# Grouped-query attention over a cached sequence on one core: the output in two PSUM banks, two copies and one store of whole rows

## The chip, the cores and the metric

The kernel runs on one NeuronCore of a Trainium2 chip. The metric is the device time of one execution in microseconds (us). Besides that time there is a profile of one execution, taken by the hardware profiler; its span runs from the first to the last instruction and is a little shorter than the time of the same execution.

The core has these engines: TensorE (PE, with its weight loads as PEld), VectorE (DVE), ScalarE (ACT), GpSimd (POOL) and SyncE (SP), which here only issues transfers. SBUF is the memory of 128 partitions that all engines read; PSUM, in eight banks per partition, receives what TensorE computes.

## The reference

```python
B, Sq, D = 8, 4, 512
Hq, Hkv, Sk, Dh = 32, 8, 2048, 128
rep = Hq // Hkv                                    # 4 query heads share a head of K and V
q = (x @ wq).reshape(B, Sq, Hq, Dh).transpose(0, 2, 1, 3)
k = jnp.repeat(k_cache, rep, axis=1)
v = jnp.repeat(v_cache, rep, axis=1)
scores = jnp.einsum("bhqd,bhkd->bhqk", q, k) * (Dh ** -0.5)
p = softmax(scores, axis=-1)
o = jnp.einsum("bhqk,bhkd->bhqd", p, v)
return o.transpose(0, 2, 1, 3).reshape(B, Sq, Hq * Dh) @ wo
```

Everything is bf16. The caches are 33.6 MB each, wq and wo 4.2 MB each; x and the output are 32 rows (8 sequences of 4 tokens) of 512 columns, 32 KB.

## The kernel before

The work is cut into 8 units: two groups of four K/V heads, times four pairs of sequences. For each unit the kernel loads 4 MB of K and 4 MB of V into one of four slots of a ring in SBUF (`load_kv`), turns K with VectorE's transposes (`turn`), computes the scores into a tile `s_ps` of four PSUM banks (`scores`), takes the maximum (`top`) and the exponentials (`exps`), turns the weights (`weights`) and multiplies them by V (`values`). The results of a unit are scaled, joined and sorted by tokens (`scaled`, `joined`, `by_tokens`). When a group of heads is complete, `to_rows` copies it out of two PSUM tiles, the first half with ScalarE, the second with VectorE, into one SBUF tile, and turns it into `oP[gg]`, in which each of 16 steps r holds 128 rows of the last product's inner dimension by 32 tokens.

The last product is `project`: for each step r and each half of the 512 output columns it multiplies `oP[gg][:, r, :]` (128 x 32) by 256 columns of wo. The first half goes to partitions 0 to 31 and the second to partitions 32 to 63 of `out_ps`, which is a view of bank 0 of `s_ps`, 256 columns wide; each half is a sum over 32 matmuls. wo is the last load, in seven pieces that get smaller towards the end (`load_wo`, L113), so that the last matmuls wait for a piece of 128 KB. Then one ScalarE copy (L409) brings the 64 x 256 sums as bf16 into `out_sb`, and SP issues one transfer (L411) that writes them. Since the halves of a row lie on different partitions, this transfer names the output as 2 x 32 rows of 256 columns, 512 bytes each.

Instructions are issued in the order of the program on each engine's own queue; an engine waits on semaphores that a planner derives from the tiles that instructions read and write. SP's queue holds all but two of the loads, and the store behind them. The waits in that queue (for a slot of the ring to come free) set when loads start. Nothing comes behind the store but the end of the program (L437 in the profile).

Of the kernel before, what the change touches and what calls it, by code (L numbers as in the profile page):

```python
# [8 lines left out]
BF16 = mybir.dt.bfloat16  # L9
# [8 lines left out]
def kernel(  # L18
# [9 lines left out]
    nc = tc.nc  # L28

    B, Sq, D = x.shape  # L30
# [4 lines left out]
    T = B * Sq  # L35
# [14 lines left out]
    DH = D // 2  # L50
# [6 lines left out]
    const = ctx.enter_context(tc.tile_pool(name="const", bufs=1))  # L57
# [19 lines left out]
    q_bd = [const.tile([128, NB, J * 2, G, NB, Q], BF16, name=f"q_bd{i}") for i in range(2)]  # L77
    p_bd = [const.tile([128, CH // 2, G, 32, 2], BF16, name=f"p_bd{i}") for i in range(4)]
    oP = [const.tile([128, RW, T], BF16, name=f"oP{i}") for i in range(NG)]
    out_sb = const.tile([2 * T, DH], BF16, name="out_sb")  # L80

    units = [(gg, bp) for gg in range(NG) for bp in range(NP)]
    slot_of = {}
# [67 lines left out]
    for r, b in ((r, b) for r in range(rep) for b in range(NB)):  # L151
        nc.gpsimd.tensor_copy(
            out=perm[:, r, 32 - NB * Sq :]
            .rearrange("k (g x) -> k g x", g=G)[:, :, : NB * Sq]
            .rearrange("k g (b s) -> k b g s", b=NB)[:, b],
            in_=by_row[:, r, b],
        )
    for b in range(NB):
        nc.vector.tensor_reduce(
            out=of_b[:, b : b + 1],  # L160
            in_=ident[:, :].rearrange("k (g b q) -> k b g q", g=G, b=NB)[:, b],
# [27 lines left out]
    s_ps = psum_s.tile([128, NT, 512], FP32, name="s_ps")  # L189
# [138 lines left out]
    def project(gg, r0, r1):  # L328
        w = ring[:, slot_of["wo"], gg, :].rearrange("p (r j) -> p r j", r=RW)
        for r in range(r0, r1):  # L330
            for half in range(2):
                nc.tensor.matmul(
                    out_ps[half * T : (half + 1) * T, :],
                    lhsT=oP[gg][:, r, :],
                    rhs=w[:, r, half * DH : (half + 1) * DH],
                    start=(gg == 0 and r == 0),
                    stop=(gg == NG - 1 and r == RW - 1),
                )
# [9 lines left out]
    for gg in range(NG):  # L348
        psq = psum_o.tile([128, rep * Dh], FP32, tag="o", name="psq")
        for r in range(R):  # L350
# [10 lines left out]
            out=q_sb[:, gg, :, :, :, :].rearrange("t r j w e -> t (r j w e)"), in_=psq[:, :]  # L361
        )
        for i in range(rep):
            nc.vector.transpose(  # L364
                out=qT[:, gg, :, :, i, :, :].rearrange("w j b s e -> w j b (s e)").bitcast(FP32),
                in_=q_sb[:, gg, i, :, :, :].rearrange("t j w e -> t (j w e)").bitcast(FP32),
            )
    queries(0)

    out_ps = s_ps[: 2 * T, 0, :DH]  # L370
    for u in range(NU + 1):
        if u < NU:
            for t in range(NT):
# [19 lines left out]
        if u >= 1:  # L393
# [5 lines left out]
            if u == NU:  # L399
                joined(u - 1)  # L400
                by_tokens(u - 2)
        issue(2 + 2 * u)
    project(0, 0, 4)
    by_tokens(NU - 1)
    to_rows(NG - 1, RW // 4)
    project(0, 4, RW)
    project(1, 0, RW)
    assert not loads
    nc.scalar.copy(out=out_sb[:, :], in_=out_ps)  # L409
    rows = out.flatten_outer_dims().rearrange("t (h n) -> h t n", h=2)  # L410
    nc.sync.dma_start(out=rows, in_=out_sb[:, :])  # L411


# [28 lines left out]
```

## Time and profile before

| | us |
|---|---|
| three runs | 185.8, 191.71, 191.63 (median 191.63) |
| profiled execution, its own time | 185.8 |
| span of the profiled execution | 183.9 |
| PE busy | 133.3 (72% of the span) |
| DVE busy | 127.3 (69%) |
| ACT busy | 74.1 (40%) |
| POOL busy | 37.7 (20%) |
| HBM read | 75.53 MB, 411 GB/s over the span |
| ScalarE's copy of the output, L409 | 0.366 |
| SP's issue of the store, L411 | 0.675 |

The mean granted TensorE clock of the profiled execution is 0.976. The times of the engines add up instructions that run beside each other; what sets the end is read from the chain of waits, which follows the last instruction back to what released it, and from the transfers.

These are the rows of the projection, by line: durations in ns (smallest, median, largest), first and last start in us, operand shapes.

```profile
L332 PEld LDWEIGHTS <-oP x64: 92/97/97, 175.3 to 179.9; 128*32 128x32 bf16 x64
L332 PE MATMUL s_ps<-ring,oP x64: 269/273/283, 175.3 to 179.9; 128*32 128x256 bf16 x64
```

The 64 matmuls of both groups stand between 175.3 and 179.9 us; the spacing of their starts is much closer than the duration of one, since they are pipelined.

### The profile page before, as it was taken

The page shows a single profiled execution, that of the slowest core. Times are in us where ns is not written, and L with a number is a line of the kernel's source. Part 1 is how long each engine was busy: PE and PEld are TensorE (multiplying, and loading weights), DVE is VectorE, ACT ScalarE, POOL GpSimd, SP SyncE. Part 2 cuts the span into 40 slices and gives each one's busy share as a digit, 9 for nine tenths or more (in the row PEclk, how much of TensorE's full clock was granted, in tenths as well). Part 3 has the DMA queues.
Part 4 walks back from the last instruction along what each step waited for, and adds up shares of the span by engine and source line. Part 5 has one row for each costly group of instructions (what it writes and reads, how often), then busy time and mean ns, then how long its engine had stood idle before and what let it go on. Part 6 is the DMA issues. An engine that isn't in the chain of part 4 may idle for free.

```text
span 183.9 us, 2334 instructions
## 1 busy us (share of the span) xinstructions
PE 133.3 (72%) x900; PEld 81.4 (44%) x900; DVE 127.3 (69%) x160; ACT 74.1 (40%) x91; POOL 37.7 (20%) x98
## 2 busy tenths in 40 slices
PE   0000079901999699978996898789788968899991
PEld 0000023300358335833782377238633853398870
DVE  6527029068975997499749965997898579769140
ACT  2000020049506940793099009902980297037010
POOL 8700033008001700260034004300520040005000
PEclk9999999995699999999999999999999999999997
DMA  6999999999999999999999999999999999999980
GB/s 271 410 435 420 435 421 438 424 438 438 424 435 421 435 424 440 417 440 435 424 431 420 442 424 433 442 413 438 420 442 428 431 435 420 421 426 424 428 316 8
DMA packets 6109, 75.71 MB, mean 412 GB/s; under 512 B 498, under 2 KB 850, under 8 KB 1106
## 3 DMA queue, kind: packets, MB, share of 16 engines
q1 hardware_dynamic: 5810, 71.37, 91.1%
q10 hardware_dynamic: 288, 4.19, 5.4%
q8 instruction: 7, 0.11, 0.2%
q14 instruction: 4, 0.03, 0.0%
HBM read 75.53 MB, written 0.03 MB: 411 GB/s over the span
## 4 chain that ended last, share of the span: by engine, by line
DVE 37%; DMA 25%; PE 19%; ACT 9%; issue 3%; SPq 2%; POOL 2%; DVEq 0%; ACTq 0%; POOLq 0%
DVE kt L172 23%; DMA ring<-in_wo_dram 14%; PE s_ps L195 13%; DMA ring<-in_wq_dram 11%; ACT p_sb L229 8%; DVE stat L208 8%; PE o_ps L269 4%; DVE pt L243 2%; DVE stat L260 2%; PE psq L353 2%; SPq L113 2%; POOL p_bd L253 1%; DVE stat L216 1%; DVE o_sb L287 1%; POOL q_bd L184 1%
## 5 line engine op out<-in xcount | busy, mean ns | idle before, releaser
L195 PE MATMUL s_ps<-kt,q_bd 128*128 128x512 bf16 x256 | 67.4, 395 | 24.3 <-POOL q_bd L184 16.3
L172 DVE STREAM_TRANSPOSE kt<-ring 128x1024 f32<-128x1024 f32 x64 | 73.8, 1207 | 5.5 <-DMA ring<-in_k_cache_dram 5.2
L269 PE MATMUL o_ps<-ring,p_bd 128*128 128x256 bf16 x512 | 57.0, 273 | 0.0
L195 PEld LDWEIGHTS <-q_bd 128*128 128x128 bf16 x256 | 24.7, 99 | 66.1 <-issue 23.6
L269 PEld LDWEIGHTS <-p_bd 128*128 128x128 bf16 x512 | 49.8, 98 | 5.9
L229 ACT ACTIVATE p_sb<-s_ps,stat 128x1024 bf16<-128x1024 f32 x16 | 22.0, 1399 | 65.3 <-DVE stat L216 65.3
L253 ACT COPY p_bd<-pt 32x1024 bf16<-32x1024 bf16 x44 | 45.8, 1041 | 1.3 <-DVE pt L243 0.8
L253 POOL COPY p_bd<-pt 32x1024 bf16<-32x1024 bf16 x16 | 17.0, 1063 | 112.0 <-DVE pt L243 109.5
L208 DVE TENSOR_REDUCE stat<-s_ps 128x1 f32<-128x1024 f32 x16 | 18.8, 1219 | 12.2 <-PE s_ps L195 12.2
L243 DVE STREAM_TRANSPOSE pt<-p_sb 128x512 f32<-128x512 f32 x16 | 11.4, 711 | 16.1 <-ACT p_sb L229 16.0
L184 POOL COPY q_bd<-qT 32x64 bf16<-32x64 bf16 x64 | 13.1, 230 | 19.4 <-DVE qT L364 17.6
L344 PE MATMUL xtp<-ident,x_sb 32*128 32x32 bf16 x4 | 0.3, 194 | 14.1 <-DMA x_sb<-in_x_dram 14.1
L353 PE MATMUL psq<-ring,xT_sb 128*32 128x512 bf16 x32 | 3.6, 629 | 8.2 <-DMA ring<-in_wq_dram 8.2
L364 DVE STREAM_TRANSPOSE qT<-q_sb 128x64 f32<-128x64 f32 x8 | 1.2, 213 | 8.9 <-ACT q_sb L360 8.9
L146 DVE MEMSET p_bd<- 128x2048 uint32 x3 | 5.3, 1765 | 2.0 <-PEq L426 1.2
L344 PEld LDWEIGHTS <-x_sb 32*128 32x128 bf16 x4 | 0.2, 117 | 14.1 <-DMA x_sb<-in_x_dram 14.1
L260 DVE TENSOR_SCALAR stat<-of_b,stat 128x2 f32<-128x2 f32 x8 | 5.9, 733 | 0.3
L287 DVE SCALAR_TENSOR_TENSOR o_sb<-o_ps,stat,o_sb 128x128 bf16<-128x128 f32 x8 | 2.5, 316 | 4.8 <-ACT o_sb L281 4.8
L353 PEld LDWEIGHTS <-xT_sb 128*32 128x32 bf16 x32 | 1.3, 139 | 9.7 <-issue 9.2
L360 ACT CAST q_sb<-psq 128x512 bf16<-128x512 f32 x2 | 1.2, 586 | 10.9 <-PE psq L353 10.9
L281 ACT ACTIVATE o_sb<-o_ps,stat 128x128 bf16<-128x128 f32 x8 | 2.9, 368 | 5.6 <-PE o_ps L269 5.4
L347 ACT COPY xT_sb<-xtp 128x128 bf16<-128x128 bf16 x1 | 0.3, 266 | 11.5 <-PE xtp L344 11.5
(26 smaller groups left out, 38.4 us busy)
## 6 DMA issues: line engine op xcount, KB each, us to landing
ring<-in_k_cache_dram SPq DMA_DIRECT2D x6, 4096.0 KB, 22.0
ring<-in_v_cache_dram SPq DMA_DIRECT2D x5, 4096.0 KB, 25.3
ring<-in_v_cache_dram SPq DMA_DIRECT2D x6, 2048.0 KB, 27.1
ring<-in_k_cache_dram SPq DMA_DIRECT2D x3, 2048.0 KB, 25.4
ring<-in_wo_dram SPq DMA_DIRECT2D x3, 1024.0 KB, 25.6
ring<-in_k_cache_dram ACTq DMA_DIRECT2D x1, 2048.0 KB, 12.1
ring<-in_wq_dram ACTq DMA_DIRECT2D x1, 2048.0 KB, 20.2
ring<-in_wq_dram SPq DMA_DIRECT2D x1, 2048.0 KB, 20.9
```

Source lines behind the costliest of these rows:

```text
L146: nc.vector.memset(t[:, :, :, :, :], 0.0)
L172: nc.vector.transpose(out=kt[:, :, :, :, :].rearrange("w c j s e -> w (c j s e)").bitcast(FP32), in_=ring[:, slot_of["k", u], b, t * n : ( ...
L184: nc.gpsimd.tensor_copy(out=qb[rows, b, :, g, b, :].rearrange("w (j e) q -> w j e q", e=2), in_=qT[rows, gg, :, NB * bp + b, :, :, :].rear ...
L195: nc.tensor.matmul(s_ps[:, t, :], lhsT=q_bd[u % 2][:, b, 2 * j + e, :, :, :].rearrange("w g b q -> w (g b q)"), rhs=kts[u, b, t][:, :, j, ...
L208: nc.vector.tensor_reduce(out=stats[u][0][:, h : h + 1], in_=s_ps[:, 2 * h : 2 * h + 2, :].rearrange("q t n -> q (t n)"), axis=AX, op=ALU.max,
L229: nc.scalar.activation(out=p_sb[:, :, :, :].rearrange("q c s e -> q c e s"), in_=s_ps[:, 2 * h : 2 * h + 2, :].rearrange("q t (c e s) -> q ...
L243: nc.vector.transpose(out=pt[:, :, :, :].rearrange("s c q e -> s (c q e)").bitcast(FP32), in_=ps[u, h][:, :, :, :].rearrange("q c s e -> q ...
L253: copy(out=pb[rows, :, g, :, :], in_=pt[rows, :, :, :])
L260: nc.vector.tensor_scalar_mul(stats[u][3][:, :], of_b[:, :], stats[u][4][:, :])
L269: nc.tensor.matmul(o_pss[u][:, :, :], lhsT=pbs[u, h][:, i // 2, :, :, i % 2].rearrange("s g q -> s (g q)"), rhs=v[:, :, h * CH + i, :], st ...
L287: nc.vector.scalar_tensor_tensor(out=o_sb[:, 1, :], in0=o_pss[u][:, 1, :], scalar=stats[u][3][:, 1:2], in1=o_sb[:, 0, :], op0=ALU.mult, op ...
L353: nc.tensor.matmul(psq[g * T : (g + 1) * T, :], lhsT=xT_sb[:, r, :], rhs=w[:, (gg * G + g) * rep * Dh : (gg * G + g + 1) * rep * Dh], star ...
```

## The change

`out_ps` becomes a list of two views: the first half stays on partitions 0 to 31 of bank 0 of `s_ps`, the second goes to partitions 32 to 63 of bank 1. `out_sb` becomes 32 rows of 512 columns. ScalarE copies the first half into its left columns, VectorE the second half (from partitions 32 to 63 to partitions 0 to 31) into its right columns, and one transfer writes 32 rows of 1024 bytes.

```diff
-    out_sb = const.tile([2 * T, DH], BF16, name="out_sb")
+    out_sb = const.tile([T, D], BF16, name="out_sb")
...
                 nc.tensor.matmul(
-                    out_ps[half * T : (half + 1) * T, :],
+                    out_ps[half],
                     lhsT=oP[gg][:, r, :],
...
-    out_ps = s_ps[: 2 * T, 0, :DH]
+
+    out_ps = [s_ps[h * T : (h + 1) * T, h, :DH] for h in range(2)]
...
-    nc.scalar.copy(out=out_sb[:, :], in_=out_ps)
-    rows = out.flatten_outer_dims().rearrange("t (h n) -> h t n", h=2)
-    nc.sync.dma_start(out=rows, in_=out_sb[:, :])
+    nc.scalar.copy(out=out_sb[:, :DH], in_=out_ps[0])
+    nc.vector.tensor_copy(out=out_sb[:, DH:], in_=out_ps[1])
+    nc.sync.dma_start(out=out.flatten_outer_dims(), in_=out_sb[:, :])
```

In the changed kernel the three last statements are lines L410, L411 and L412.

## The prediction

> **What bounds the kernel now.** I read the page first (span, busy tenths, transfer rate), then the end of the chain of waits, then the timeline, the queue's waits and the transfers of the last microseconds, because the change touches only what stands behind the last matmuls.
>
> The page:
>
> ```profile
> span 183.9 us, 2334 instructions
> ...
> DMA  6999999999999999999999999999999999999980
> GB/s 271 410 435 420 435 421 438 424 438 438 424 435 421 435 424 440 417 440 435 424 431 420 442 424 433 442 413 438 420 442 428 431 435 420 421 426 424 428 316 8
> DMA packets 6109, 75.71 MB, mean 412 GB/s; under 512 B 498, under 2 KB 850, under 8 KB 1106
> ```
>
> From the second slice to the third from the end the transfer engines are busy at 410 to 442 GB/s: the kernel is bound by reading its 75.5 MB, and nothing in the change reads a byte more or less. Only the last slice moves almost nothing (8 GB/s). The chain of waits from 179 us on:
>
> ```profile
> 153.61 25.58 DMA ring<-in_wo_dram
> 179.19 0.04 issue
> 179.23 0.62 PE s_ps L332 x6
> 179.85 0.01 issue
> 179.86 0.30 PE s_ps L332 x2
> 180.16 0.02 issue
> 180.19 0.37 ACT out_sb L409
> ```
>
> The last piece of wo lands, eight matmuls of 256 columns finish the output, ScalarE copies it. Then the timeline (start, duration), SP's own waits, and the transfers of the window 181 to 183.9 us (40 slices of 0.0725 us):
>
> ```profile
> 180.58 0.68 SPq L411 DMA_DIRECT2D out_dram<-out_sb  x1
> ```
>
> ```profile
> SPq L437 <- DMA out_dram<-out_sb: 1.5, 1, 1.5
> ```
>
> ```profile
> DMA  0000000000001101111111110000000000000000
> GB/s 0 0 0 0 0 0 0 0 0 0 0 7 28 14 14 42 42 49 42 42 42 42 42 42 0 0 0 0 0 0 0 0 0 0 0 0 0 0 0 0
> DMA packets 66, 0.03 MB, mean 11 GB/s; under 512 B 2, under 2 KB 66, under 8 KB 66
> ```
>
> So the tail behind the last matmul is 180.16 to 183.91, 3.75 us: hand-over and copy 0.42, issue 0.68, 0.54 until the first packet (slice 11, 181.80), packets until slice 23 ends (182.74, so 0.94), and 1.17 for the last hand-over and the barriers that close the program. The store runs on few transfer engines: the busy share is one tenth of 16, at 42 GB/s. The two packets under 512 B say how few. The program has 31 loads, and the page counts 498 such short packets: 31 x 16 + 2. I read them as one completion write for each transfer engine that takes part, 16 for every load, also for x (32 rows of 1024 bytes), and 2 for this store of 2 x 32 rows of 512 bytes. So 64 packets go through two engines, 32 in a row each, at 0.94 / 32 = 29 ns.
>
> **The change, part by part.** All against the profiled execution, whose own time is 185.8 us: span 183.9 and 1.9 around it. The median of the three runs shown is 191.63; two of them lie within 0.1 of it, 5.9 us above the profiled one, and no trace shows where. The change's difference is worked out in the profiled one and carried over to both.
>
> *Two banks.* The second half's matmuls go to the next bank, on the same 32 partitions as before. Number, shapes and order of PE's instructions stay, and so do their waits. The two halves already lie on different partitions, and in the stretch of 41 such matmuls at 176.73 they come every 2.46 / 41 = 60 ns, under the 97 ns of a weight load: two streams overlap now. Only the last pair is in the open; it could gain at most one such step (0.06) or lose a whole matmul if pairs stopped overlapping (0.27). I take 0, since pace and operands are the same. Both banks were last read for these columns by L229 of the last unit, from 163.74 to 165.14, ten microseconds before the first write at 175.34.
>
> *Copies.* ScalarE's copy keeps 256 columns; with 128 partitions (L321) it takes 0.372, with 64 (L409) 0.366, so with 32 it stays at 0.37. VectorE gets a copy of 256 columns from PSUM, whose nearest row is:
>
> ```profile
> L321 DVE CAST q_sb<-o_pm_e x2: 416/420/425, 127.7 to 176.5; 128x256 bf16<-128x256 f32 x2
> ```
>
> 0.42 us. It reads partitions 32 to 63 and writes 0 to 31, which no row does; L321's 0.42 is the nearest, and the 0.35 of the 128-column L287 bounds it below. Do the copies run side by side? In the order of the changed kernel's instructions, VectorE's copy (now L411) waits for ScalarE's counter alone, at 74, the value that the copy of L410 sets; and the store waits for VectorE's. So they run one after the other. Behind VectorE's wait stands only the end of the program (its last transposes ended at 178.4); SP, with the store, waits for it. Hand-over from ScalarE to VectorE: 0.03 (L281 ends at 175.64, L287 starts at 175.67). Added to the path: 0.03 + 0.42 = 0.45. If they overlapped, VectorE alone would end at 180.61 instead of 180.56: 0.05.
>
> The Trainium skill, page "PSUM — Partial Sum Buffer", section "Specifications (TRN2)", says that ScalarE and VectorE can read PSUM in parallel at full rate as long as their banks differ; by that alone the added term would be 0.05, not 0.45. Nothing in the trace before has two such copies on one output, and the listed wait decides for me.
>
> *Issue.* SP's issue of the old store took 0.675. The nearest row for the new one is the load of x, of the very same 32 rows of 1024 bytes on both sides: 0.406 (all loads of the ring that waited for nothing: 0.33 to 0.61). I take 0.41: a gain of 0.27, bounds 0 and 0.34.
>
> *Transfer.* 32 packets of 1024 bytes on 16 engines, as for x: two each. The step of 29 ns for 512 bytes gives 58 for 1024, two of them 0.12; the first packets are slower (7 to 28 GB/s in the first four slices), so I take 0.20. A gain of 0.74; bounds 0.12 (gain 0.82) and 0.94 (gain 0). From the end of the issue to the first packet: 0.54 for the store, 0.5 for the first load of k (issued until 1.12, packets from about 1.65): unchanged, as are the closing 1.17.
>
> *SBUF.* out_sb takes 1024 bytes of a partition for 512, and the buffers placed behind it move. Nothing in the rows tells addresses apart: 0.
>
> Sum: + 0.45 - 0.27 - 0.74 = - 0.56 us. Copies until 181.01, issue 181.03 to 181.44, packets 181.98 to 182.18, end 183.35. That is 185.2 for the profiled execution, and 191.1 for the median.
>
> **The rivals.**
> 1. *The store gets no shorter, and the serial copy stays* (slower). If issue and landing hang on one round trip to memory and not on the number of packets, the new copy's 0.45 is paid and nothing comes back: 186.25, or 192.1 for the median. It decides when issue and packets together shrink by less than 0.45 of their 1.62. For it: of the 2.16 us from issue to landing only 0.94 hold packets. Against it: the packets visibly come one behind the other for 0.94, on two engines. 0.15. The page "DMA: Bandwidth & Descriptors" of the Trainium skill, section "Anatomy of one DMA — SWDGE (gpsimd) path", has this rule: some 2.0 us fixed for any transfer, mostly the wait for the written bytes' receipt, plus bytes at 436 GB/s. An estimate by that page is 2.08 us for 32 KB in either shape. The trace's 2.16 is close to it in sum but not in its parts, so I give it no more.
> 2. *The copies overlap after all*, if the wait named is met earlier than its line suggests: -0.96, so 184.8 or 190.7. 0.05, since 74 is the last count of ScalarE.
> 3. *The run's level, not the kernel.* The three runs lie at 185.8, 191.71 and 191.63. If the runs after lie mostly at the lower level, the median falls to about 185.2, 3.4% below 191.63 (0.17); if the comparison sets a higher level after against the lower one before, it reads 191.1 against 185.8, 2.9% up (0.10). Nothing in the diff acts on such a level, since the 178 us of loads are the same.
>
> **How the numbers follow.** My forecast, a gain of about 0.56 us (0.3%) at the level of the median shown, has 0.53; rivals 1 and 2 have 0.15 and 0.05 and stay within 2%, which is about what a measurement of this kernel can tell from no change. 2% of 185.8 is 3.7 us, about the whole tail: a mechanism in it would have to remove the tail to make the kernel faster by that much, and to double it to make it slower. So over 2% comes from rival 3 alone: faster 0.17, slower 0.10, within 0.73. Time: 191.1. The forecast's own range: 190.6 to 192.1 at that level (rival 2's end and the bound of rival 1), and 184.8 to 186.3 at the profiled one. The range has to hold both levels: 184.8 to 192.1.
>
> **What would show it.** In the changed profile: 512 packets under 512 B instead of 498; a store of 32 packets of 1024 bytes within 0.2 us at over 100 GB/s; issue near 0.41; VectorE's copy starting 0.03 behind the end of ScalarE's and taking 0.42; matmuls and loads as before. The prediction is wrong if the packets still take 0.9 us (rival 1), if the copies start together (rival 2), or if the time before 179 us moves by more than the tail does, which none of my steps could explain.

## The result and the profile after

| | before | after |
|---|---|---|
| median of 10 runs each, us | 185.65 | 185.08 |
| ratio of the runs compared | 1 | 0.9969, 95% interval 0.9960 to 0.9978 |
| span of the profiled execution, us | 183.9 | 183.2 |
| end of the last matmul to the end of the span, us | 3.75 | 3.18 |

The change gains 0.31%, about 0.58 us; the tail behind the last matmul is 0.57 us shorter. Over a quarter of all runs, some of every kernel here, lie 4 to 7 us higher, two of the three runs shown at first among them; such runs are left out of the ratios, and where a profile below is of one (e1 and e6, spans 191.7 and 190.1) only its tail is read.

The page of the changed kernel:

```profile
span 183.2 us, 2335 instructions
...
DMA packets 6092, 75.71 MB, mean 413 GB/s; under 512 B 513, under 2 KB 833, under 8 KB 1089
```

One instruction more (VectorE's copy), and 15 short packets more than before: the store's 2 have become 16, and one more lies elsewhere. The chain of waits of the changed kernel at its end (start, duration, what):

```profile
153.51 25.57 DMA ring<-in_wo_dram
179.08 0.04 issue
179.12 0.63 PE s_ps L332 x6
179.75 0.01 issue
179.76 0.30 PE s_ps L332 x2
180.06 0.02 issue
180.08 0.37 ACT out_sb L410
180.46 0.02 issue
180.48 0.42 DVE out_sb L411
```

Up to the last matmul it is the chain of before, 0.10 us earlier. Then VectorE's copy stands behind ScalarE's, 0.02 after its end, and adds 0.44. The timeline (start, duration, in brackets what the engine waited for) and SP's waits of the changed kernel:

```profile
180.48 0.42 DVE L411 CAST out_sb<-s_ps 32x256 bf16<-32x256 f32 x1 [2.15 <-ACT out_sb L410]
180.92 0.35 SPq L412 DMA_DIRECT2D out_dram<-out_sb  x1
```

```profile
SPq L438 <- DMA out_dram<-out_sb: 0.9, 1, 0.9
```

The store is issued 0.34 later than before (180.58), but its issue takes 0.35 instead of 0.68, so both kernels end it at the same time, 181.27 and 181.26. From there SP waits 0.9 instead of 1.5. Why, the transfers in the window 180.3 to 183.2 us show (40 slices of 0.0725 us):

```profile
DMA  0000000000000000000058410000000000000000
GB/s 0 0 0 0 0 0 0 0 0 0 0 0 0 0 0 0 0 0 0 0 113 198 99 43 0 0 0 0 0 0 0 0 0 0 0 0 0 0 0 0
DMA packets 48, 0.03 MB, mean 11 GB/s; under 512 B 16, under 2 KB 48, under 8 KB 48
```

Up to eight tenths of the transfer engines are busy at up to 198 GB/s, for four slices (0.29 us), where two engines took 0.94 at 42 GB/s. Of the 48 packets 32 hold data and 16 are short: by the reading in the prediction, one short packet per engine that takes part.

So in a sum: copies + 0.44 (with the hand-over), issue - 0.33, wait for the first packet - 0.06, packets - 0.65, closing barriers about + 0.03. That is - 0.57 in the tail. The last three terms are read from slices and are good to about one slice, 0.07.

### The profile page after: what moved, and what is told of

It is laid out like the page before. It is cut to its first block, busy times and chain, and to the rows that moved or that the text cites. A ratio compares the mean times of both kernels' runs of the same rounds, so it can differ in the third digit from the quotient of the medians.

```text
span 183.2 us, 2335 instructions
## 1 busy us (share of the span) xinstructions
PE 132.7 (72%) x900; PEld 81.2 (44%) x900; DVE 127.8 (70%) x161; ACT 74.1 (40%) x91; POOL 37.6 (21%) x98
## 3 DMA queue, kind: packets, MB, share of 16 engines
q10 hardware_dynamic: 288, 4.19, 5.4%
## 4 chain that ended last, share of the span: by engine, by line
DVE 42%; DMA 25%; PE 15%; ACT 10%; issue 4%; SPq 2%; DVEq 0%; ACTq 0%
DVE kt L172 27%; DMA ring<-in_wo_dram 14%; DMA ring<-in_wq_dram 11%; ACT p_sb L229 9%; PE s_ps L195 8%; DVE stat L208 8%; PE o_ps L269 4%; DVE stat L260 3%; DVE pt L243 2%; SPq L113 2%; PE psq L353 2%; DVE stat L216 1%; DVE o_sb L287 1%; DVE stat L259 1%; PE s_ps L332 1%
## 5 line engine op out<-in xcount | busy, mean ns | idle before, releaser
L195 PE MATMUL s_ps<-kt,q_bd 128*128 128x512 bf16 x256 | 66.7, 391 | 24.9 <-POOL q_bd L184 16.3
L287 DVE SCALAR_TENSOR_TENSOR o_sb<-o_ps,stat,o_sb 128x128 bf16<-128x128 f32 x8 | 2.5, 315 | 4.8 <-ACT o_sb L281 4.8
```

The source lines that it names most:

```text
L195: nc.tensor.matmul(s_ps[:, t, :], lhsT=q_bd[u % 2][:, b, 2 * j + e, :, :, :].rearrange("w g b q -> w (g b q)"), rhs=kts[u, b, t][:, :, j, ...
L287: nc.vector.scalar_tensor_tensor(out=o_sb[:, 1, :], in0=o_pss[u][:, 1, :], scalar=stats[u][3][:, 1:2], in1=o_sb[:, 0, :], op0=ALU.mult, op ...
```

## The experiments

The theory: three parts act one by one on the tail, VectorE's copy (+ 0.44), the issue and the number of transfer engines of the store (together about - 1.0), and the second bank does nothing. The rivals take the store's gain from its longer rows, or the copies from something that hides them, or give the second bank a share. Ratios are to the kernel before on the same chip; the tail is from the end of the last matmul to the end of the span of the one profiled execution. The expected times start from 185.65 for the kernel before and 185.08 for the changed one; beside the experiments the kernel before took 185.81 and 185.84, so what is to be compared with an expectation is the distance to the kernel before, not the time.

| | ratio, 95% interval | in us of 185.8 | tail, us | tail against 3.75 |
|---|---|---|---|---|
| the change | 0.9969 (0.9960 to 0.9978) | - 0.58 | 3.18 | - 0.57 |
| e1 store of 2 x 16 rows | 1.0022 (1.0013 to 1.0032) | + 0.41 | 4.23 | + 0.48 |
| e6 store of 4 x 8 rows | 1.0008 (0.9997 to 1.0018) | + 0.15 | 3.92 | + 0.17 |
| e5 banks and copies alone | 1.0024 (1.0012 to 1.0035) | + 0.45 | 4.19 | + 0.44 |
| e3 one bank | 0.9966 (0.9952 to 0.9979) | - 0.63 | 3.18 | - 0.57 |
| e4 two tiles in PSUM | 0.9942 (0.9928 to 0.9957) | - 1.08 | 2.83 | - 0.92 |
| e7 the two tiles alone | 1.0001 (0.9991 to 1.0010) | + 0.02 | 3.77 | + 0.02 |
| e2 one copy, two stores | 0.9953 (0.9939 to 0.9966) | - 0.87 | 2.83 | - 0.92 |
| e8 ScalarE copies both | 0.9963 (0.9949 to 0.9977) | - 0.69 | 3.10 | - 0.65 |

The tails of single profiles follow the times within 0.16 us throughout, so the tail accounts for all but that; the largest difference, e4's 0.16, was not traced.

**e1 and e6: fewer engines, same rows.** The changed kernel, with the output's rows named in another order, so that the outermost count of the store's pattern is 2 (e1, shown here) or 4 (e6, `a=4`); the rows are written in that order, which isn't the reference's.

```diff
-    nc.sync.dma_start(out=out.flatten_outer_dims(), in_=out_sb[:, :])
+    nc.sync.dma_start(out=out.flatten_outer_dims().rearrange("(t a) n -> a t n", a=2), in_=out_sb[:, :])
```

> The changed kernel, but its store names the output as 2 x 16 rows of 1024 bytes (rows 0, 2, 4, ... and then 1, 3, 5, ...), so the 32 rows are written in another order than the reference has; bytes, rows of 1024 and the number of data packets (32) stay. Theory (the gain of the store comes from the number of transfer engines, which the outermost count of the pattern limits): 2 packets under 512 B instead of 16, 16 data packets in a row on each of two engines at 46 to 58 ns, so 0.74 to 0.93 us of packets instead of 0.29, issue back near 0.68 instead of 0.35; 185.08 + 0.45 to 0.64 + 0.33 = 185.9 to 186.1. Rival (the gain comes from rows of 1024 instead of 512 bytes, or half as many packets): packets stay at about 0.3 us and the time at 185.1.

> As e1, but the store names the output as 4 x 8 rows of 1024 bytes (rows 0, 4, 8, ..., then 1, 5, 9, ...; again written in another order than the reference's). Theory (engines times about 18 GB/s each): 4 short packets, 8 data packets in a row on each engine, about 0.45 us of packets, issue about 0.7; behind the last matmul 0.4 less than e1's 4.2 us, 3.8. Rival (the pattern of three dimensions is what costs, not the count of engines): as e1, 4.2 us behind the last matmul and 0.9 us of packets.

Measured: e1 186.23 and e6 186.00 as medians of the runs compared, the kernel before beside them 185.81 and 185.84. The transfers of the last 3 us (slices of 0.075 us), e1:

```profile
DMA  0000000000000110101111110000000000000000
GB/s 0 0 0 0 0 0 0 0 0 0 0 0 14 41 27 0 27 27 55 55 41 41 55 55 0 0 0 0 0 0 0 0 0 0 0 0 0 0 0 0
DMA packets 34, 0.03 MB, mean 11 GB/s; under 512 B 2, under 2 KB 34, under 8 KB 34
```

and e6:

```profile
DMA  0000000000000000002222220000000000000000
GB/s 0 0 0 0 0 0 0 0 0 0 0 0 0 0 0 0 0 27 68 55 55 82 82 68 0 0 0 0 0 0 0 0 0 0 0 0 0 0 0 0
DMA packets 36, 0.03 MB, mean 11 GB/s; under 512 B 4, under 2 KB 36, under 8 KB 36
```

The short packets are 2 and 4, as many as the outermost count, and the busy share is one tenth and two tenths (2 and 4 of 16 engines would be 0.125 and 0.25). The packets take twelve slices (0.90 us) with two engines and seven (0.53) with four, mostly at 41 to 55 and 55 to 82 GB/s. Over the whole stretch each engine moves some 16 to 18 GB/s with 8, 16 or 32 packets to itself (e6, e1 and the kernel before); with two packets each on 16 engines, in the changed kernel, it is only 7 (32 KB in 0.29 us), so the time doesn't shrink in proportion to the engines. Two engines need as long for 32 rows of 1024 bytes as for the 64 of 512 in the kernel before (0.94), so the rows' length isn't what the change gains by, and e1's rival falls. The issue took 0.76 and 0.80: with four engines no shorter than with two. What makes it long, fewer engines than 16 or source and destination cut differently, stays open; a pattern of three dimensions alone isn't enough, since the loads of K and V have three too and issue in about 0.37 (median, kernel before). So e6's tail is 0.31 shorter than e1's where 0.4 was expected; its ratio alone doesn't set it apart from the kernel before.

**e5: banks and copies alone.** The kernel before with the two banks and the two copies, but out_sb of 64 rows and the old store.

```diff
-    nc.scalar.copy(out=out_sb[:, :], in_=out_ps)
+    nc.scalar.copy(out=out_sb[:T, :], in_=out_ps[0])
+    nc.vector.tensor_copy(out=out_sb[T:, :], in_=out_ps[1])
     rows = out.flatten_outer_dims().rearrange("t (h n) -> h t n", h=2)
     nc.sync.dma_start(out=rows, in_=out_sb[:, :])
```

> The kernel before with only the first two parts of the change: two banks and two copies (ScalarE the first half into rows 0 to 31 of out_sb, VectorE the second into rows 32 to 63), and the old store of 2 x 32 rows of 512 bytes. VectorE's copy waits for ScalarE's. Theory (the copy in series is a full term of its own, and the store keeps its two engines): 185.65 + 0.44 = 186.1, slower than the kernel before; 2 short packets, packets over 0.94 us. Rival (the copy is hidden behind something, so that the changed kernel's gain is the store's alone): 185.65.

Measured 186.25 (before beside it 185.84). The end of its chain of waits:

```profile
179.92 0.30 PE s_ps L332 x2
180.22 0.02 issue
180.24 0.37 ACT out_sb L410
180.61 0.02 issue
180.64 0.42 DVE out_sb L411
```

The series of the changed kernel, 0.44 behind ScalarE's copy, and nothing that hides it. The store still has 2 short packets, and its issue takes 0.67. This half of the change is a loss of its own. With - 0.58 for the whole, the store's part is then - 0.58 - 0.45 = - 1.03, against - 1.01 from the trace (0.33 + 0.65 + 0.06 - 0.03).

**e3: one bank.** The changed kernel with both halves in bank 0.

```diff
-    out_ps = [s_ps[h * T : (h + 1) * T, h, :DH] for h in range(2)]
+    out_ps = [s_ps[h * T : (h + 1) * T, 0, :DH] for h in range(2)]
```

> The changed kernel with both halves in bank 0 (partitions 0 to 31 and 32 to 63). Theory (the second bank does nothing by itself: PE's pace is the same in both profiles, and the copies run in series either way): 185.1, last two matmuls 0.30, chain behind the last matmul as in the changed kernel. Rival (two banks speed up PE or the copies): slower than the changed kernel by 0.1 or more.

Measured 185.13, tail 3.18 as with two banks. Its chain of waits at the last matmuls:

```profile
179.12 0.62 PE s_ps L332 x6
179.73 0.00 issue
179.73 0.30 PE s_ps L332 x2
180.03 0.02 issue
180.06 0.37 ACT out_sb L410
180.43 0.02 issue
180.45 0.42 DVE out_sb L411
```

The same durations as in the changed kernel, within 0.01: the second bank does nothing here, and isn't what makes the copies wait for each other either.

**e4 and e7: the copies side by side.** In e4 `s_ps` of the changed kernel becomes two tiles of two banks each, with one half of the output in each; e7 makes the same two tiles in the kernel before.

```diff
-    s_ps = psum_s.tile([128, NT, 512], FP32, name="s_ps")
+    s_ps = [psum_s.tile([128, 2, 512], FP32, name=f"s_ps{h}") for h in range(2)]
...
-                        s_ps[:, t, :],
+                        s_ps[t // 2][:, t % 2, :],
...
-            in_=s_ps[:, 2 * h : 2 * h + 2, :].rearrange("q t n -> q (t n)"),
+            in_=s_ps[h][:, :, :].rearrange("q t n -> q (t n)"),
...
-    out_ps = [s_ps[h * T : (h + 1) * T, h, :DH] for h in range(2)]
+    out_ps = [s_ps[h][h * T : (h + 1) * T, 0, :DH] for h in range(2)]
```

> The changed kernel with s_ps as two tiles of two banks each, and one half of the output in each tile; VectorE's copy then waits for PE and no longer for ScalarE, and the store waits for both copies. Theory (the copies are in series only because both read one tile in the planner's books, and VectorE's copy is a full 0.44 on the path): both copies start within 0.05 of each other, the store is issued 0.39 earlier, 185.08 - 0.39 = 184.7. Rival (two engines at PSUM hold each other up, or the store's start is set by something else): 185.1. The split also lets the maximum and the exponentials wait for two banks instead of four; since the loads set the pace I expect under 0.1 of that at the end.

> The kernel before with s_ps as two tiles of two banks, and nothing else: what e4 has beside the change. Theory (the loads set the pace, so earlier maxima and exponentials are worth nothing at the end): 185.65, and behind the last matmul 3.75 us. Rival (part of e4's gain over the changed kernel comes from the split itself and not from the copies side by side): faster than the kernel before by 0.1 or more.

Measured: e4 184.78 (before 185.81), e7 185.81 (before 185.84). The timeline of e4:

```profile
180.31 0.36 ACT L410 CAST out_sb<-s_ps 32x256 bf16<-32x256 f32 x1 [3.43 <-PE s_ps L332]
180.34 0.42 DVE L411 CAST out_sb<-s_ps 32x256 bf16<-32x256 f32 x1 [1.78 <-PE s_ps L332]
180.82 0.35 SPq L412 DMA_DIRECT2D out_dram<-out_sb  x1
```

Both copies now wait for PE, start 0.03 apart and take what they took in series: the two engines don't hold each other up. The two tiles lie in different banks; whether copies out of one bank would run side by side as well, no run shows. The store is issued 0.50 behind the last matmul (180.32) instead of 0.86. The tail is 0.35 shorter than the changed kernel's (0.39 expected; the store starts 0.06 behind the later copy instead of 0.02), and the intervals of e4 (five runs) and of the change, each against its own runs of the kernel before, don't overlap. Against e3, which has the changed kernel's tail and ran beside e4, the medians are 0.35 apart as well (185.13 and 184.78), though these two intervals overlap slightly. e7's 1.0001 says that the two tiles alone are worth nothing, so the gain is the overlap. The wait was the planner's, which orders accesses by the tile, not the chip's. e4 is the version whose interval lies clear of both kernels'.

**e2: one copy, two stores.** The kernel before with its single copy; SP and ScalarE's queue each store one half, 32 rows of 512 bytes.

```diff
-    rows = out.flatten_outer_dims().rearrange("t (h n) -> h t n", h=2)
-    nc.sync.dma_start(out=rows, in_=out_sb[:, :])
+    rows = out.flatten_outer_dims()
+    nc.sync.dma_start(out=rows[:, :DH], in_=out_sb[:T, :])
+    nc.scalar.dma_start(out=rows[:, DH:], in_=out_sb[T:, :])
```

> The kernel before (one bank, one ScalarE copy of 64 x 256, rows of 512 bytes), but the store is cut into two of 32 rows of 512 bytes, one issued by SP and one by ScalarE's queue. Theory (number of engines): each store has 16 short packets, 32 in all, both issue in about 0.35 us side by side, data packets within 0.3 us; against the kernel before it gains issue 0.33 and packets 0.65: 185.65 - 0.98 = 184.65, below the changed kernel, since VectorE's copy in series (0.44) isn't there. Rival (rows of 1024 bytes are what makes the store short): 185.6.

Measured 184.94. Its last 3 us of transfers (slices of 0.075 us):

```profile
DMA  0000000000000000002583000000000000000000
GB/s 0 0 0 0 0 0 0 0 0 0 0 0 0 0 0 0 0 0 55 110 178 89 7 0 0 0 0 0 0 0 0 0 0 0 0 0 0 0 0 0
DMA packets 96, 0.03 MB, mean 11 GB/s; under 512 B 32, under 2 KB 96, under 8 KB 96
```

Rows of 512 bytes on 16 engines (twice 16 short packets) are through in four slices, with little left for a fifth, about as fast as rows of 1024: the rival falls a second time. The gain is 0.9, not the expected 1.0: the copy came as expected and both stores were issued at 180.65, but ScalarE's issue took 0.39, 0.04 longer than SP's, and from its end (181.04) to the end of the span it took 2.02, against 1.97 in the changed kernel. These account for the tail; the remaining 0.05 between tail and time wasn't traced. Its tail equals e4's, and the two versions' intervals overlap.

**e8: ScalarE does both copies.**

```diff
-    nc.vector.tensor_copy(out=out_sb[:, DH:], in_=out_ps[1])
+    nc.scalar.copy(out=out_sb[:, DH:], in_=out_ps[1])
```

> The changed kernel, but ScalarE does both copies, one after the other, with no wait between them. Theory (what counts is the sum of the copies in a row, and the hand-over between engines is 0.02 to 0.03): second copy 0.36 instead of 0.02 + 0.42, or less if ScalarE overlaps two copies; 185.08 - 0.08 to - 0.2 = 184.9 to 185.0. Rival (ScalarE pays something between two copies that VectorE hides): 185.1 or more.

Measured 185.17; the copies start at 180.27 and 180.64, each 0.36, tail 3.10. As a time this would fall to the rival (185.1 or more), but it is 0.67 below the kernel before beside it, within what the theory expects. By the tail the 0.08 of the theory is there; the time (interval 0.9949 to 0.9977) can't tell it from the change. Two copies on one engine were no worse than two engines in series.

## Why the prediction was right and where it was wrong

*The difference.* Forecast - 0.56, measured - 0.58 (ratio) and - 0.57 (tail). Term by term: VectorE's copy with its hand-over 0.45, measured 0.44 (180.46 to 180.90), and e5 shows it as a loss by itself; ScalarE's copy 0.37, measured 0.36; the second bank 0, e3 shows 0; the issue 0.41, measured 0.35, so this gain was 0.33 instead of 0.27; the packets 0.20, measured 0.29, so that gain was 0.65 instead of 0.74; issue to first packet 0.54, measured 0.48; the closing 1.17, measured 1.20. The misses (- 0.01, - 0.06, + 0.09, - 0.06, + 0.03) add up to - 0.01: the terms and their signs were right, but that the sum is right to a hundredth is luck. The largest miss is the packets' term: steps scaled from the old store, with 0.08 added for a slow start, gave 0.20 where 0.29 was measured. The "0.35" of L287 that bounds VectorE's copy below is the last of eight that take 0.30 to 0.35; nothing hung on it.

*The reading behind the store's term.* That the two odd short packets mean two engines was read from a count (31 x 16 + 2); e1, e6 and e2 bear it out with 2, 4 and 2 x 16 short packets, and the first two with the busy shares and times that go with 2 and 4 engines. The Trainium skill has the rule, page "DMA: Bandwidth & Descriptors", section "Why a DMA increments its semaphore by 16 and not by 1": a transfer uses the largest number of engines up to 16 that divides the slowest dimension that isn't 1 on both sides. By that the old store (64 rows in SBUF, 2 x 32 rows outside) and e1's have 2, e6's 4 and the new store 16; the short packets agree in every case.

*The rivals.* The first, a store that gets no shorter and a serial copy that remains, decides when issue and packets shrink by less than 0.45: they shrank by 0.98. Its mechanism is there in half, as e5: 0.45 slower. From the start of the issue to the last packet the old store took 2.16 us and the new one, by the same parts, 0.35 + 0.48 + 0.29 = 1.12, so the time was not fixed. The Trainium skill's section with the 2.0 us has fitted it to transfers that GpSimd issues; these two stores are SP's. The second rival, copies that overlap, did not happen, and e4 shows that nothing in the chip forbids it; the sentence of the Trainium skill's page "PSUM — Partial Sum Buffer" that both engines read at full rate from different banks agrees with e4's 0.36 and 0.42. The wait that the built program lists, and not that rate, set the time of the changed kernel.

*The step that failed* is the one that turned a difference into a time: "The median of the three runs shown is 191.63 ... The change's difference is worked out in the profiled one and carried over to both", with 191.1 as the number given. That is 6.0 above the measured 185.08, and set beside the 185.65 that the kernel before takes as the median of ten runs it would even be a loss of 5.45 us. The sum's own end, 185.2, was the right forecast, 0.12 off: every term came from the profiled execution, which is next to that median, and three runs that lie 5.9 us apart don't say which of them is the kernel's level. The range held 185.08 only because it reached over both levels. Rival 3, a median after at about 185.2, is what came, and had been given a chance of 0.17.

## What to carry to other kernels

A small store at the end of a kernel is worth a look at its short packets and its busy share: a pattern whose outermost count is 2 kept 14 of 16 transfer engines idle here, and naming whole rows, or cutting the store into two of 32 rows, brought them in. Splitting a copy over two engines gains nothing, and cost 0.44 here, while both read one tile by the planner's account; look at what each copy waits for in the order of the built program, and give each half its own tile. Price a change against the execution that the terms come from, and give that level unless many runs say otherwise.

## What had not been expected of the hardware

The issue of a store that runs on 2 or 4 engines held SP for 0.67 to 0.80 us, of one on 16 engines for 0.35, with the same 32 KB. And with 16 engines the data packets take about 0.3 us however they are cut (32 of 1024 bytes, 64 of 512 in two stores), while SP's wait for the landing, from the end of its issue, is 0.8 to 0.9 us in the changed kernel, e2, e3, e4 and e8 alike: nothing that was tried here got below that.
